# Attention, gated block and top-2 experts on one core: PV in threes, 400 slots per expert, and unequal early parts

## The chip, the cores and the metric

The kernel runs on one core of a Trainium2 chip. The metric is the device time of one execution in microseconds, as the median of several runs. Three executions of the kernel before took 881.61, 883.17 and 885.46 us.

## The reference, cut to what matters

Three blocks follow each other. Every matmul works on 32-bit values; weights and activations are split into a rounded high part and a low remainder, so that a product costs three matmuls (high x high, low x high or high x low, in the order the kernel chooses).

```python
# 1. attention, 2 x 8 heads, 768 positions, 64 wide; a score counts only within a hash bucket
scores = where(q_bucket == k_bucket, scale * q @ k.T, -1e9)
attn = exp(scores - max); attn /= sum(attn) + 1e-9
x = attn @ v                                   # 1536 tokens x 512
# 2. gated block, 512 -> 2048 -> 512
h = x @ w_in; x = (h * clip(h + 3, 0, 6) / 6) @ w_out
# 3. top-2 of 8 experts, 512 -> 1024 -> 512
noisy = x @ w_gate + log1p(exp(x @ w_noise)) * noise
for e in range(8):
    out[mask] += weight * (relu(x[mask] @ w1[e]) @ w2[e])   # mask: tokens with e in their top 2
```

`w_in` and `w_out` come as 64-bit floats.

## The kernel before, in words

TensorE (PE), VectorE (DVE), ScalarE (ACT) and GpSimd (POOL) carry out their instructions in the order of the program, which is written out by hand; SyncE (SP) issues most DMAs, also in that order, as soon as the buffer that a DMA writes is free. So the order of the Python loops is the order on each engine.

**Attention** (about 0 to 244 us). Two heads are worked on together, in 8 pairs p, each in two half-blocks of queries (`hb`), each with 6 key tiles of 128. The main loop (L609) runs over 96 steps g; 12 steps are a pair, 6 a half-block. Step g issues the scores of step g + 1 (`scores`, L470: for each of two heads two 384-wide matmuls into a tile "S", of which there are two, and an exponential on ACT into one of four tiles E), between them two or three `maxes` (L430: matmuls into one of two double tiles "mx", then a DVE reduce), and in every odd step the products with V of two key tiles (`av`, L482: 24 small matmuls each with half of the array's columns). After that come, in this order: the loads and splits of later pairs, the sum of V (`v_sum`, L324, at the ninth step of a pair: a POOL memset, then a DVE reduce), one step of the conversion, the weights of the next block, and what was deferred to this step (`at`, `run_deferred`): the stabiliser's transpose, eviction and DMA (`stab2`, L459, from the ACT queue, behind the third step of a half-block), the V-sum matmul (`v_sum2`), the uniform term (`uniform`, POOL), and the end of a half-block (`finish`).

**Conversion** (`conv`, L188). The 64-bit weights are turned into 32-bit ones in 32 pieces, 16 of them in attention: a load c_raw into a buffer of tag "wr", three steps later two ACT passes and a DVE pass, then DVE and POOL, DVE, and a store. Its buffers are those of the weights: "wr", "wh" and "wl", three each. `conv_step` (L670) moves every started piece by one stage and starts a new one where g % 6 == 3. The first three weight tiles are loaded in steps 84 to 86 (L676) and cast in 88 to 91.

**Gated block** (244 to 523 us). 48 units (3 chunks of 512 tokens x 16 slices of 128 hidden columns). A unit loads 512 KB of weights (`w_load`), casts them (`w_hi`, ACT) and takes the rest (`w_lo`, DVE), multiplies (`gemm1`, 12 matmuls; `gemm2`, 12 matmuls of 512 columns). Gates and top 2 are worked out per chunk (`routing`), and each token's row of 516 floats is scattered to a slot of its expert in DRAM (`xg`).

**Experts.** The slots of expert e are rows of `xg`, CAP of them. An expert has 8 units of 128 hidden columns with 512 KB of weights each. `PARTS` (L30) lists the work in order: expert, first slot, slots, row tiles, swapped or not. Experts 0 and 1 have an early part whose slots are filled by the first two chunks, so that it can run while the third chunk is routed (this stretch, 523 to 583 us, is called the passage); the rest of their slots comes last. A swapped part (`sw`) keeps weights stationary in the second layer too: 12 + 12 matmuls a unit as wide as the part has slots, into four banks (two tiles "S"), then four copies into `yt` and transposes back (`e_back`, four per row tile). A part that is not swapped has in the second layer, for each row tile, three matmuls of 512 columns a unit into half of one tile "S", and `e_out` scales the result and adds it to the output by a scattering DMA. In that form, the second row tile's matmuls of the last unit write the same tile that the first's `e_out` reads. `e_load`, `e_meta`, `e_trans` gather, read and transpose the slots of the next part in given units of the one before (`EL1`, L1074); expert 2's gather is issued by POOL, in column pieces, after the third chunk's scatter; later ones by SP at the first unit of the part before. If an expert got more than CAP rows, a block at the end (L1097) works off the rest.

Of the kernel before, what the change touches and what calls it, by code (L numbers as in the profile page):

```python
# [8 lines left out]
F32 = mybir.dt.float32  # L9
# [7 lines left out]

BIG = float(2 ** 33)
HALF = float(2 ** 32)
CAP = 416  # L20
EARLY = (224, 224)
ROW = 516
PF = (8, 2)
NU = 16
NS = 2
CL = 3
SL = CAP // 4
ROUTE = [(3, 0, 0), (1, 1, 0), (0, 1, 0), (5, 0, 0)]
NQ = len(EARLY)
PARTS = ([(e, 0, n, 2, False) for e, n in enumerate(EARLY)] + [(e, 0, CAP, 4, True) for e in range(NQ, 8)]  # L30
         + [(e, n, CAP - n, 2, False) for e, n in enumerate(EARLY)])
FSPLIT = 7
XA = 5
QJ = (1, 5)
# [10 lines left out]
def chain_kernel(ctx, tc, kq, vP, proj, wm, we, wgn, noise, out, dbg=None):  # L45
# [237 lines left out]
    with actx:  # L283
# [12 lines left out]
        def at(g, f, *a):  # L296
            defer.setdefault(g, []).append((f, a))
# [184 lines left out]
        def av(g):  # L482
            p, qh, kt = g // (2 * KT), g // KT % 2, g % KT
            t = T[p]
            if kt == 0:
                t["av"] = ps.tile([128, 512], F32, name="o", tag="o", bufs=1)
            for h in range(2):
                for i in range(KT // 2):
                    c = (h * (KT // 2) + i) * VW
                    for r in (0, 64):  # L490
                        nc.tensor.matmul(t["av"][r:r + 64, c:c + VW],  # L491
                                         E[g % NE][:, h, i * 128 + r:i * 128 + r + 64], t["V"][:, kt, h],
                                         start=kt == 0 and h == 0 and i == 0, stop=kt == KT - 1,
                                         tile_position=(0, r), skip_group_check=True)
            if kt == 0:
                at(g + 1, uniform, 2 * p + qh)
            elif kt == KT - 1:
                at(g + 1, finish(p, qh, t["av"]))

# [103 lines left out]
            elif i == 7:  # L603
                low_q(1)
        v_sum(0, False)
        at(0, v_sum2, 0)
        pend = []
        soon = []
        for g in range(G):  # L609
            p, j = divmod(g, 2 * KT)  # L610
            hb, st = divmod(g, KT)
            ahead = done[0] - ((hb + 2) * NI + 2 * st)
            todo = more(3 if ahead < 0 else 2, hb + 3)
            for hbd in pend:
                stab(hbd)
            pend2, pend = pend, []
            sc = scores(g + 1) if g + 1 < G else iter(())
            for k in range(2):
                next(sc, None)
                if todo:  # L620
                    m = todo.pop(0)
                    maxes(*m)
                    if m[1] == NI - 1:
                        pend.append(m[0])
                while soon:
                    f = soon.pop()
                    f[0](*f[1:])
            next(sc, None)
            if g in XG:
                x_split(0, [XG.index(g)])  # L630
            if g == G - 1:
                m1_first(0)
            if g % 2:
                av(g - 1)
                av(g)
            while todo:
                m = todo.pop(0)
                maxes(*m)
                if m[1] == NI - 1:
                    pend.append(m[0])  # L640
            for hbd in pend2:
                d = 2 if hbd > 2 else 0
                at(g + d, stab2, hbd)
            if p + 2 < NP:
                if j == 0:
                    load_cast(p + 2)
                elif j == 4:
                    bits_all(p + 2)
                    soon.append((bits_all2, p + 2))
                    at(g + 1, bits_all3, p + 2)  # L650
                    move_q(p + 2)
                elif j in (6, 7):
                    lows(p + 2, j - 6)
                elif j == 8:
                    move_mask_all(p + 2)
            if p + 1 < NP:
                if j == QJ[0]:
                    with tc.issue_after(T[0]["nrd"].ins):
                        move_qx(p + 1)
                elif j == QJ[1]:  # L660
                    move_k(p + 1)
            if p >= 1 and p + 1 < NP and j == 2:
                load_v(p + 1)
            if p + 1 < NP and j == 8:
                v_sum(p + 1)
                at(g + 3, v_sum2, p + 1)
            if p + 3 < NP and j == 6:
                load_raw(p + 3)
            if dbg is None or "x" not in dbg:
                conv_step(1 if g % 6 == 3 and cvn[0] < NU else 0, None, True)  # L670
            if g == 14:
                moe_consts()
            elif g == 16:
                moe_gate(f_p)
            if G - 12 <= g < G - 9:
                w_load(g - G + 12)  # L676
            elif g in WG:
                k = WG.index(g)
                (w_hi, w_lo)[k % 2](k // 2)
            run_deferred(g)  # L680
# [16 lines left out]
    def gemm2(y, k, gh, gl, m, first, last, ts=range(4)):  # L697
        wh, wl = W[k][1][:, 512:], W[k][2][:, 512:]
        for t in ts:
            o = y[t // 2][:m, t % 2, :]  # L700
            c = slice(t * m, (t + 1) * m)
            nc.tensor.matmul(o, gh[:, c], wh, start=first, stop=False)  # L702
            nc.tensor.matmul(o, gh[:, c], wl, start=False, stop=False)  # L703
            nc.tensor.matmul(o, gl[:, c], wh, start=False, stop=last)  # L704

    def m1_second(u):
        c, ft = plan[u]
        if ft in (0, FSPLIT):
            ys["y", c] = [ps.tile([128, 2, 512], F32, name="S", tag="S", bufs=2) for _ in range(2)]
        gh, gl = ys.pop(("g", u))  # L710
        y = ys["y", c]
        gemm2(y, u, gh, gl, 128, ft in (0, FSPLIT), ft in (FSPLIT - 1, 15))
        W.pop(u)
        if ft == FSPLIT - 1:
            if c < 2:
                ye = ys["ye", c] = x_rows(c)
            else:
                ye = ys["ye", c] = m_p.tile([128, 4, ROW], F32, name="ye", bufs=1)
            nc.scalar.copy(ye[:, 0:2, 0:512], y[0])
            nc.scalar.copy(ye[:, 2:4, 0:512], y[1])  # L720
        elif ft == 15:
            for i in range(2):
                yd = ys["ye", c][:, 2 * i:2 * i + 2, 0:512]
                nc.vector.tensor_tensor(yd, y[i], yd, op=ALU.add)
# [209 lines left out]
    def m2_second(v):  # L934
        q, ft = divmod(v, 8)
        e, s0, n, nt, sw = PARTS[q]
        if ft == 0:
            ex["y", q] = [ps.tile([128, 2, 512], F32, name="S", tag="S", bufs=2) for _ in range(2 if sw else 1)]
        hh, hl = ex.pop(("h", v))
        y = ex["y", q]  # L940
        if not sw:
# [3 lines left out]
            for t in range(nt):  # L945
                gemm2(y, NMU + v, hh, hl, n // nt, ft == 0, ft == 7, (t,))
                if ft == 7:
                    e_out(q, t, y[0][:, t, :])
        else:
            wh, wl = W[NMU + v][1:]  # L950
            for d in range(4):
# [235 lines left out]
```

## Time and profile before

| | us |
|---|---|
| median of three runs | 883.17 |
| profiled execution, its own time | 878.66 |
| its span | 876.8 |
| TensorE busy | 829.8 (95%) |
| weight loads into TensorE | 717.1 (82%) |
| VectorE busy | 524.4 (60%) |
| ScalarE busy | 422.2 (48%) |
| GpSimd busy | 214.5 (24%) |

The profile tells of one execution. TensorE's matmuls are pipelined: the time of one in a row is longer than the step from one start to the next, so the price of a matmul is read from two starts. In a timeline a row gives start, duration, engine, line, operation, out<-in, shape and count; brackets give the idle time before it and what ended it. Several matmuls of one kind in a row are merged into one row.

### The profile page before, as it was taken

The page shows a single profiled execution, that of the slowest core. Times are in us where ns is not written, and L with a number is a line of the kernel's source. Part 1 is how long each engine was busy: PE and PEld are TensorE (multiplying, and loading weights), DVE is VectorE, ACT ScalarE, POOL GpSimd, SP SyncE. Part 2 cuts the span into 40 slices and gives each one's busy share as a digit, 9 for nine tenths or more (in the row PEclk, how much of TensorE's full clock was granted, in tenths as well). Part 3 has the DMA queues.
Part 4 walks back from the last instruction along what each step waited for, and adds up shares of the span by engine and source line. Part 5 has one row for each costly group of instructions (what it writes and reads, how often), then busy time and mean ns, then how long its engine had stood idle before and what let it go on. Part 6 is the DMA issues. An engine that isn't in the chain of part 4 may idle for free.

```text
span 876.8 us, 15979 instructions
## 1 busy us (share of the span) xinstructions
PE 829.8 (95%) x6313; PEld 717.1 (82%) x6313; DVE 524.4 (60%) x865; ACT 422.2 (48%) x714; POOL 214.5 (24%) x244
## 2 busy tenths in 40 slices
PE   7899999999799999999999999989999999999993
PEld 3677788788678888888878787879999999999982
DVE  7678777777356776645556557555445444544651
ACT  5455455456446666644444444443444444343551
POOL 6345444343211311100040124410112020211211
PEclk9999999999899999999999999999999999999997
DMA  8667668661345799862252265973565555645661
GB/s 259 174 187 211 185 161 235 170 177 56 117 156 188 221 319 317 302 229 97 73 184 90 92 207 164 293 203 124 152 169 134 162 131 164 136 147 145 174 196 22
DMA packets 52348, 151.75 MB, mean 173 GB/s; under 512 B 8741, under 2 KB 9661, under 8 KB 52265
## 3 DMA queue, kind: packets, MB, share of 16 engines
q1 hardware_dynamic: 44393, 131.02, 48.3%
q0 software_dynamic: 7648, 19.53, 10.2%
q8 instruction: 51, 0.84, 0.4%
q14 instruction: 32, 0.26, 0.1%
q10 hardware_dynamic: 224, 0.10, 0.0%
HBM read 105.89 MB, written 32.41 MB: 158 GB/s over the span
## 4 chain that ended last, share of the span: by engine, by line
PE 79%; DVE 8%; DMA 3%; issue 3%; ACT 3%; POOL 2%; POOLq 0%; ACTq 0%; SPq 0%; DVEq 0%
PE mx L260 28%; PE o L491 7%; PE S L702 5%; PE S L704 5%; PE S L703 5%; PE S L954 4%; PE S L955 4%; PE S L956 4%; PE S L477 4%; PE mx L440 3%; PE S L478 3%; DVE mc L444 2%; DVE wl L238 1%; DVE vr L329 1%; ACT wh L232 1%
## 5 line engine op out<-in xcount | busy, mean ns | idle before, releaser
L238 DVE TENSOR_TENSOR wl<-wr,wh 128x1024 fp32r<-128x1024 f32 (+1 forms) x128 | 155.6, 1216 | 126.6 <-ACT wh L232 124.9
L232 ACT CAST wh<-wr 128x1024 fp32r<-128x1024 f32 x128 | 134.3, 1049 | 123.8 <-PE S L956 75.6
L479 ACT ACTIVATE E<-S 128x384 f32<-128x384 f32 x192 | 90.3, 491 | 82.5 <-PE S L478 76.7
L444 DVE TENSOR_REDUCE mc<-mx 128x1 f32<-128x768 f32 x96 | 90.3, 953 | 32.8 <-PE mx L440 32.8
L982 POOL DMA_INDIRECT out_dram<-ot,ti x28 | 44.1, 1575 | 234.9 <-ACT ot L981 186.1
L276 DVE SCALAR_TENSOR_TENSOR g<-t,mx 128x512 f32<-128x512 f32 x47 | 32.4, 689 | 94.6 <-ACT t L275 94.6
L702 PE MATMUL S<-wh,gh 128*128 128x512 f32 (+1 forms) x208 | 82.1, 395 | 1.1 <-ACT xh L919 1.1
L491 PEld LDWEIGHTS o<-V,E 128*64 128x64 f32 x2304 | 72.7, 140 | 12.3 <-issue 9.6
L477 PE MATMUL S<-QX,KS 128*128 128x384 f32 x192 | 75.7, 394 | 6.2 <-ACT E L479 6.0
L704 PE MATMUL S<-wh,gl 128*128 128x512 f32 (+1 forms) x208 | 81.1, 390 | 0.0
L703 PE MATMUL S<-wl,gh 128*128 128x512 f32 (+1 forms) x208 | 81.0, 389 | 0.0
L491 PE MATMUL o<-V,E 128*64 128x66 f32 x2304 | 79.4, 226 | 0.0
L440 PE MATMUL mx<-B,A 128*128 128x384 f32 x192 | 64.6, 349 | 11.8 <-DVE mc L444 9.3
L954 PE MATMUL S<-hh,wh 128*128 128x416 f32 x192 | 70.7, 368 | 0.0
L955 PE MATMUL S<-hh,wl 128*128 128x416 f32 x192 | 67.5, 352 | 0.0
L956 PE MATMUL S<-hl,wh 128*128 128x416 f32 x192 | 67.4, 351 | 0.0
L478 PE MATMUL S<-A,B 128*128 128x384 f32 x192 | 65.6, 342 | 1.4 <-DMA A<-mr 1.4
L929 ACT ACTIVATE hh<-mx 128x416 fp32r<-128x416 f32 (+2 forms) x72 | 33.0, 459 | 66.1 <-PE mx L260 65.7
L260 PE MATMUL mx<-xh,wh 128*128 128x512 f32 (+1 forms) x252 | 61.8, 367 | 2.8 <-ACT wh L232 2.8
L260 PE MATMUL mx<-xh,wl 128*128 128x512 f32 (+1 forms) x252 | 60.8, 363 | 1.8 <-DVE wl L238 1.6
L275 ACT ACTIVATE t<-mx,half 128x512 f32<-128x512 f32 x47 | 32.3, 688 | 59.2 <-PE mx L260 59.2
L260 PE MATMUL mx<-xl,wh 128*128 128x512 f32 (+1 forms) x252 | 60.2, 360 | 0.0
(247 smaller groups left out, 1588.9 us busy)
## 6 DMA issues: line engine op xcount, KB each, us to landing
wr<-in_we_dram SPq DMA_DIRECT2D x80, 512.0 KB
wr<-w SPq DMA_DIRECT2D x48, 512.0 KB
c_raw<-in_wm_dram SPq DMA_DIRECT2D x32, 512.0 KB
xg<-pt SPq DMA_DIRECT2D x8, 838.5 KB
raw<-in_kq_dram SPq DMA_DIRECT2D x8, 768.0 KB
B<-in_kq_dram POOLq DMA_DIRECT2D x7, 768.0 KB, 9.7
xr<-xg SPq DMA_DIRECT2D x5, 838.5 KB
w<-c_ta SPq DMA_DIRECT2D x16, 256.0 KB
```

The lines of the kernel that those rows point to most:

```text
L232: nc.scalar.copy(hi, W[k][0])
L238: nc.vector.tensor_tensor(lo[:, :n], W[k][0][:, :n], W[k][1][:, :n].bitcast(F32), op=ALU.subtract)
L260: nc.tensor.matmul(h, a[:, d * 128:(d + 1) * 128], b[:, d], start=i == 0 and d == 0, stop=i == 2 and d == 3)
L444: nc.vector.tensor_reduce(t["mc"][:, c:c + 1], pm[:, :, :QW], axis=AX.XY, op=ALU.max)
L477: nc.tensor.matmul(s[:, :QW], t["KS"][:, h, ks], t["QX"][:, qh, qs], start=True, stop=False)
L491: nc.tensor.matmul(t["av"][r:r + 64, c:c + VW], E[g % NE][:, h, i * 128 + r:i * 128 + r + 64], t["V"][:, kt, h], start=kt == 0 and h == 0 ...
L702: nc.tensor.matmul(o, gh[:, c], wh, start=first, stop=False)
L703: nc.tensor.matmul(o, gh[:, c], wl, start=False, stop=False)
L704: nc.tensor.matmul(o, gl[:, c], wh, start=False, stop=last)
L954: nc.tensor.matmul(o, wh[:, ds], hh, start=ft == 0, stop=False)
L955: nc.tensor.matmul(o, wl[:, ds], hh, start=False, stop=False)
L956: nc.tensor.matmul(o, wh[:, ds], hl, start=False, stop=ft == 7)
```

## The change

PV is done for three key tiles in a row, in the third and sixth step of a half-block (`AV`); `uniform` moves with it, from the second to the third step. The first `v_sum2` moves from step 0 to step 1. A conversion starts every five steps instead of six, still 16 in attention. CAP falls from 416 to 400 (and the 104 partitions of whole-expert tiles to 100). Expert 0's early part keeps 224 slots; expert 1's has 128 in one row tile. At the end comes expert 1 with 272 slots, swapped, in four row tiles of 68, and after it expert 0 with 176 slots in two. In parts that are not swapped the first row tile accumulates in a tile "S", a second one in a bank of tag "mx", of which there are four.

```diff
-CAP = 416
-EARLY = (224, 224)
+CAP = 400
+EARLY = (224, 128)
...
+AV = 3
 SL = CAP // 4
...
-PARTS = ([(e, 0, n, 2, False) for e, n in enumerate(EARLY)] + [(e, 0, CAP, 4, True) for e in range(NQ, 8)]
-         + [(e, n, CAP - n, 2, False) for e, n in enumerate(EARLY)])
+PARTS = ([(0, 0, EARLY[0], 2, False), (1, 0, EARLY[1], 1, False)] + [(e, 0, CAP, 4, True) for e in range(NQ, 8)]
+         + [(1, EARLY[1], CAP - EARLY[1], 4, True), (0, EARLY[0], CAP - EARLY[0], 2, False)])
...
             if kt == 0:
-                at(g + 1, uniform, 2 * p + qh)
+                at(g + AV - 1, uniform, 2 * p + qh)
...
-        at(0, v_sum2, 0)
+        at(1, v_sum2, 0)
...
-            if g % 2:
-                av(g - 1)
-                av(g)
+            if g % AV == AV - 1:
+                for i in range(g - AV + 1, g + 1):
+                    av(i)
...
-                conv_step(1 if g % 6 == 3 and cvn[0] < NU else 0, None, True)
+                conv_step(1 if g % 5 == 3 and cvn[0] < NU else 0, None, True)
...
         for t in ts:
-            o = y[t // 2][:m, t % 2, :]
+            o = y[t][:m]
...
-        gemm2(y, u, gh, gl, 128, ft in (0, FSPLIT), ft in (FSPLIT - 1, 15))
+        gemm2([i[:, j] for i in y for j in range(2)], u, gh, gl, 128, ft in (0, FSPLIT), ft in (FSPLIT - 1, 15))
...
         if ft == 0:
-            ex["y", q] = [ps.tile([128, 2, 512], F32, name="S", tag="S", bufs=2) for _ in range(2 if sw else 1)]
+            y = [ps.tile([128, 2, 512], F32, name="S", tag="S", bufs=2) for _ in range(2 if sw else 1)]
+            if not sw:
+                y = [y[0][:, 0]] + [ps.tile([128, 512], F32, name="mx", tag="mx", bufs=MX) for _ in range(nt - 1)]
+            ex["y", q] = y
...
-                    e_out(q, t, y[0][:, t, :])
+                    e_out(q, t, y[t])
```

## Rows read from the trace of the kernel before

**Rows 1.** The page: TensorE's granted clock in 40 slices, tenths of full speed.

```profile
PEclk9999999999899999999999999999999999999997
```

**Rows 2.** Busy us by stage: length, PE, PEld, DVE, ACT, POOL; clock, DMA share, GB/s.

```profile
108.50:135.10 26.60, 25.45 (x383) 21.14 (x382) 20.49 (x28) 14.42 (x32) 11.95 (x19) 1.00 0.70 194
...
235.00:236.00 1.00, 1.00 (x4) 0.68 (x4) 0.72 (x1) 0.62 (x2) 0.18 (x1) 0.50 0.47 123
...
552.90:583.10 30.20, 27.01 (x173) 22.73 (x172) 15.93 (x26) 13.56 (x22) 6.51 (x7) 1.00 0.90 243
583.10:813.00 229.90, 229.90 (x1297) 225.95 (x1296) 112.89 (x168) 93.23 (x138) 35.60 (x23) 1.00 0.57 149
```

**Rows 3.** Timeline of TensorE in the expert stage.

```profile
803.59 0.91 PE L260 MATMUL mx<-xth,wh 128*128 128x416 f32 x4
...
805.85 0.33 PE L918 MATMUL mx<-ident,xr 96*128 96x96 f32 x2
...
840.91 0.47 PE L702 MATMUL S<-wh,hh 128*96 128x512 f32 x1 [0.77 <-ACT ot L981]
...
841.68 0.58 PE L260 MATMUL mx<-xth,wh 128*128 128x192 f32 x4
...
843.00 0.39 PE L702 MATMUL S<-wh,hh 128*96 128x512 f32 x1
...
844.38 0.58 PE L260 MATMUL mx<-xth,wh 128*128 128x192 f32 x4
```

**Rows 4.** Timeline of TensorE in attention and just after it.

```profile
109.92 0.33 PE L478 MATMUL S<-A,B 128*128 128x384 f32 x1
...
110.62 0.34 PE L440 MATMUL mx<-B,A 128*128 128x384 f32 x1
110.89 1.62 PE L491 MATMUL o<-V,E 128*64 128x66 f32 x48
112.44 0.44 PE L477 MATMUL S<-QX,KS 128*128 128x384 f32 x1
...
113.70 0.44 PE L477 MATMUL S<-QX,KS 128*128 128x384 f32 x1
...
233.53 0.69 PE L477 MATMUL S<-QX,KS 128*128 128x384 f32 x1 [4.85 <-ACT E L479]
...
236.75 2.38 PE L491 MATMUL o<-V,E 128*64 128x66 f32 x48
...
251.47 1.21 PE L260 MATMUL mx<-xh,wh 128*128 128x512 f32 x4 [1.44 <-ACT wh L232]
```

**Rows 5.** Timeline of ScalarE in the passage.

```profile
572.07 1.04 ACT L232 CAST wh<-wr 128x1024 fp32r<-128x1024 f32 x1 [4.56 <-DMA wr<-in_we_dram]
```

**Rows 6.** Timeline of SyncE at the end of attention.

```profile
227.29 5.23 SPq L191 DMA_DIRECT2D c_raw<-in_wm_dram  x2
```

**Rows 7.** Timeline of ScalarE in attention.

```profile
110.00 0.65 ACT L202 ACTIVATE c_lu<-c_raw 128x512 int32<-128x512 uint32 x1
...
111.12 0.86 ACT L479 ACTIVATE E<-S 128x384 f32<-128x384 f32 x2
113.16 1.03 ACT L479 ACTIVATE E<-S 128x384 f32<-128x384 f32 x2 [1.18 <-PE S L478]
...
114.36 0.62 ACTq L468 DMA_DIRECT2D A<-mr  x1
...
230.91 0.69 ACT L202 ACTIVATE c_lu<-c_raw 128x512 int32<-128x512 uint32 x1 [4.45 <-DMA c_raw<-in_wm_dram]
```

**Rows 8.** TensorE's waits, 28 to 214 us: total, times, longest.

```profile
PE mx L440 <- DVE mc L444: 7.2, 6, 1.7
```

**Rows 9.** Timeline of VectorE in attention: the sum of V.

```profile
129.88 1.60 DVE L329 TENSOR_REDUCE vr<-V 128x132 f32<-128x792 f32 x1 [1.44 <-POOL V L327]
```

**Rows 10.** Busy time by stretches of 1 us: gathers of 104 and of 96 partitions.

```profile
732.00:733.00 1.00, 1.00 (x9) 0.94 (x8) 0.50 (x2) 0.61 (x2) 0.00 (x0) 1.00 0.84 173
...
769.50:770.50 1.00, 1.00 (x7) 0.99 (x6) 0.00 (x0) 0.90 (x1) 0.00 (x0) 1.00 1.01 367
```

## The prediction

> **What bounds the kernel now.** I read the clock line of the page first, then the busy time by stage, then the order of TensorE's instructions inside each stage the change touches. The clock stands at full speed but for one slice [rows 1]. In the six whole experts (583 to 813 us) TensorE is busy all the time, so there a shorter matmul is a shorter kernel [rows 2]. In a middle attention period of twelve steps it is busy 25.5 of 26.6 us and VectorE 20.5 [rows 2]. In the passage (expert 1's early part, 552.9 to 583.1) it is busy 27.0 of 30.2 us while the DMA engines stand at 0.90: there TensorE waits for weights [rows 2]. The end of attention has a hole of its own.
>
> **Six experts, 416 to 400 slots.** Twelve 416-wide matmuls run from 803.59 to 805.85, 188 ns each; four 384-wide steps run from 109.92 to 110.62, 175 ns each [rows 3, 4]. So 16 columns are worth 6.7 ns. Each expert has 8 units of 24 such matmuls: 1152 x 6.7 ns = **-7.7 us**, all on the path. Weight casts and hidden-layer evictions run beside it. With the reference's inputs the experts get 364 to 396 rows, so 400 slots hold them and no overflow block runs.
>
> **The end, experts 1 and 0.** Before, two parts of 192 slots: 12 narrow matmuls take 841.68 to 843.00 (110 ns each), six 512-wide ones 843.00 to 844.38 (230 ns), so 2.70 us a unit, 43.2 for 16 [rows 3]. 192 columns do not go below 110 ns although the slope above would give 95: a floor. After, 176 slots lie on the same floor: 8 x 2.70 = 21.6. Expert 1's late part becomes 24 matmuls of 272 columns a unit. From the 175 ns at 384 the slope gives 128 ns, the floor 110; the line is nearer, since 128 is above the floor, so 8 x 24 x 128 ns = 24.6 (bound 21.1). Being swapped it is also transposed back: 16 transposes, about 0.11 us each, 1.7, and its gather needs 8 more small transposes, 0.4. On the other side, a second row tile now has a PSUM tile of its own: before, it waited for the first one's eviction (0.77 us idle and the 0.39 of a matmul where a step is 0.23: 0.93 lost), four times in the kernel, twice here [rows 3]: -1.9. Sum: 46.2 - 43.2 + 1.7 + 0.4 - 1.9 = **+3.2 us**. The gathers of the two last parts change places on SyncE, each still issued one part ahead.
> The Trainium skill ("TensorE: Matmul & The Clock Gate", Back-to-back issue gap) gives N/2.4 + 2.5 ns per warm matmul, 116 ns at 272 columns; the sum would be 2.3 us lower by it. The trace disagrees: 188 ns at 416 and 175 at 384, where the formula has 176 and 163, so I keep the line.
>
> **The passage.** Expert 1's early part drops from two row tiles to one: 24 wide matmuls fewer, 24 x 0.23 = 5.5 us if TensorE set the pace. It doesn't: ScalarE waits 4.56 us for the weights of the last unit and starts the cast at 572.07 [rows 5]. As many weights must come, and the loads of expert 2 wait for the last scatter as before, so I take this arrival as fixed. What is left is what comes after it: the second layers of the last two units (2 x 0.69) and an eviction wait like the one above (0.93) [rows 3]: **-2.3 us**; bounds 0 and -5.5. The eviction wait at the end of expert 0's early part vanishes too, but only to wait longer for weights: 0. Holding one of the four "mx" banks for that part leaves three; a unit uses two in 2.7 us and each is read within about 1 us, so 0.
>
> **The end of attention.** The last two conversions start at steps 87 and 93, while the first three weight tiles want the same three buffers. SyncE can issue the load c_raw only at 227.29; ScalarE waits 4.45 us for it at 230.91 with the exponentials queued behind; TensorE then idles 4.85 us, comes back at a granted clock of 0.50, the 1.2 GHz level (48 PV matmuls take 2.38 us against 1.62), and later waits 1.44 us for the third weight tile [rows 2, 4, 6, 7]. With a start every 5 steps the 16th conversion starts at step 78 and is stored at 87, ahead of the casts at 88; SyncE gets the same loads and stores, closer together. Removed: 4.85 + 1.44 + about 1.9 for two steps at half clock (estimate from that block and scores half as fast) = **-8.2 us**. What is late next: the second weight cast of 1.05 us comes at a step without PV followed by another, +0.8.
>
> **The middle of attention** (steps 2 to 83). Five things.
> (a) Entering PV costs 0.27 us (110.62 to 110.89) instead of 0.175 [rows 4]. Leaving it isn't shown apart; between nothing and the same again, I take the same. 16 blocks fewer of 48, some 14 of them here: -2.7.
> (b) Two score tiles rotate. In a step without PV the exponentials begin 0.72 us after the step's first matmul (112.44, 113.16), and the next step's first score waits for the first of them: a step takes 1.26 us where six matmuls and the slower first one need 1.15 [rows 4, 7]. There are 64 such steps instead of 48: +1.
> (c) The stabiliser's eviction and its DMA issue (0.62 us) sit on ScalarE behind step 2 of a half-block [rows 7]. Before, a PV step followed and hid it. Now two steps without PV follow: the issue ends 1.28 us (114.98) after the step's first score (113.70) [rows 4, 7], some 0.1 earlier where ScalarE is idle before it, and an exponential would start after 0.72: it starts 0.46 to 0.49 late and the next step waits. 12 half-blocks: +5.9; zero if ScalarE caught up.
> (d) A conversion's two ScalarE passes (110.00 to 111.12) always fell behind an even step, ahead of a PV step [rows 7]. With a period of 5 against 6 they visit all positions; in two of six (6 conversions) two steps without PV follow: the passes end some 2.9 us into the first (exponentials done at 1.7, then the passes), where the next exponentials are due at 1.26 + 0.72, so TensorE waits about 0.95: +5.7; zero to 10.
> (e) Once in 12 steps VectorE's sum of V waits 1.44 us for a POOL memset behind POOL's share of the conversion, and maxes then wait for reduces: 7.2 us in six waits [rows 8, 9]. Now the sum falls behind a PV step of some 3.5 us, the uniform term comes after the memset, and the conversion isn't locked to it: -6.9; bounds 0 and -7.2.
> Sum -2.7 + 1 + 5.9 + 5.7 - 6.9 = **+3.0 us**, bounds -9 and +10. The V-sum matmul moved out of step 0 frees TensorE while VectorE stays late: -1 (0 to -2).
>
> **Sum**: -7.7 + 3.2 - 2.3 - 8.2 + 0.8 + 3.0 - 1.0 = -12.2 us. The profiled execution took 878.66 us (span 876.8), so 866.5; the median of the runs, 883.17, lies 4.5 us above it, and I carry the difference: **871.0 us**.
>
> **Rivals.**
> 1. The new ScalarE delays don't show: c and d at zero, the middle at -8.6, total -24: 859. For: ScalarE is busy only 14.4 of 26.6 us [rows 2]. Against: its queue is in order and the two score tiles leave no slack [rows 7]. Chance 0.13.
> 2. The weights of the passage come earlier because TensorE releases buffers sooner: -5.5 there, 868. For: a load starts when a split ends. Against: the DMA engines are full [rows 2]. It shares the forecast's outcome; 0.12.
> 3. Slower: VectorE becomes the bound of attention. It has 20.5 us of work in 26.6 [rows 2], and 1.1 more by the denser conversions. If it could not use the four long PV stretches of a period, 2 us each, a period would take 21.6 + 8 = 29.6, 3.0 more; seven periods +21, in place of the middle's +3.0, so 889. It decides where reduces can't run two tiles behind the maxes. Against: each reduce takes 0.96 of a 1.26 us step. Chance 0.05.
> 4. The hole at the end of attention stays, because another load holds the weight buffers: +7.4, 878. Chance 0.1.
> 5. Expert 1's late gather has 68 partitions. During a 104-partition gather the DMA engines are 0.84 busy at 173 GB/s, during a 96-partition one 1.01 at 367 [rows 10]: a gather doesn't use them all. Were it on a quarter of them, at 140 KB an engine instead of 65 KB in about 6 us, it would take 13 us and hold up the weights queued behind it, of which three units are in flight: some 3 us late, 874. Chance 0.08. The Trainium skill ("DMA: Bandwidth & Descriptors", How many engines (k)) says that the partition count must divide by the number of engines used: 13 for 104, 10 for 100, 4 for 68; the share of 0.84 agrees with 13 of 16.
>
> **How the numbers follow.** The forecast itself has 0.52, around 866 to 876. With rivals 2, 4, 5 and part of 1, 860 to 878 holds about 8 in 10; outside lie the better half of rival 1 and rival 3. A change under 0.5% (4.4 us) is about what a measurement of this kernel can't tell from none. Faster by more: rivals 1, 2, 5, half of 4 and the forecast but for 0.03, 0.87. Within it: that 0.03 and the other half of 4, 0.08. Slower: rival 3, 0.05.
>
> **What would show it.** Right: no idle above 2 us between steps 84 and 95 and a full clock there; a unit of experts 2 to 7 0.16 us shorter (24 x 6.7 ns); expert 1's early part some 2.3 us shorter with ScalarE still waiting for weights; 272-wide matmuls near 128 ns; PV blocks of 72; after steps 3 of half-blocks a wait of about 0.5 us on the exponentials; maxes hardly waiting for reduces. Wrong: VectorE busy over 85% in the middle periods, an expert period unchanged, or weights waited for beside the 68-partition gather.

## The result, and the profile after

The changed kernel took 872.87 us (median of 8 runs, 869.03 to 880.01), the kernel before 883.4 (8 runs, 880.2 to 886.49): a ratio of 0.9884, interval 0.9856 to 0.9913, 10.5 us less. The forecast was 871.0. The profiled executions differ by less: 878.66 before, 872.92 after. The one of before lay 4.7 us under its median, the one of after lies on its own.

First the page of the changed kernel: the busy times and the clock line that answers to [rows 1].

```profile
PE 825.2 (95%) x6357; PEld 719.0 (83%) x6357; DVE 516.8 (59%) x867; ACT 424.3 (49%) x717; POOL 217.0 (25%) x245
...
PEclk8899999999999999999999999989999999999998
```

The dip at the end of attention (slice 10, counted from 0) is gone. New ones stand in the first two slices and in the passage (slice 26). Lines of the code have moved by 1, and by 4 from the experts' second layer on: L441 is the maxes' matmul, L478 and L479 the score matmuls, L480 the exponential.

Then the time by stretch, in both traces and in a second profile of the kernel before (an experiment below). A step begins with its first score matmul; in the experts a stretch begins where ScalarE starts on a unit's hidden layer:

| us | before | before, again | after | forecast of the change |
|---|---|---|---|---|
| to step 6 | 40.6 | 38.9 | 41.5 | -1.0 (start) |
| steps 6 to 83 | 173.2 | 174.3 | 179.3 | +3.0 (middle) |
| steps 84 to 93 | 25.2 | 24.6 | 19.2 | -8.2 + 0.8, with the next line's 1.44 |
| on to expert 0's first eviction | 285.1 | 287.7 | 286.5 | |
| expert 0's early part | 24.5 | 24.5 | 24.3 | 0 |
| passage, to expert 2's second unit | 37.0 | 37.0 | 34.9 | -2.3 |
| six experts, 46 of their 48 units | 225.2 | 225.2 | 218.1 | -7.4 (46/48 of -7.7) |
| on to the last matmul | 52.4 | 52.4 | 54.6 | +3.2 |
| after it | 13.6 | 13.6 | 12.7 | |

Busy time in four of these stretches of the changed kernel: an attention period of twelve steps, steps 84 to 93, the passage, the six experts (length, PE, PEld, DVE, ACT, POOL; clock, DMA share, GB/s).

```profile
111.69:139.95 28.26, 25.95 (x382) 20.97 (x382) 19.91 (x30) 15.80 (x34) 10.97 (x14) 1.00 0.72 203
220.76:239.94 19.18, 16.66 (x263) 13.19 (x262) 5.84 (x10) 11.00 (x25) 5.18 (x4) 1.00 0.20 71
550.67:585.58 34.91, 30.04 (x176) 25.93 (x175) 18.38 (x32) 15.94 (x28) 10.71 (x11) 0.90 0.94 269
585.58:803.67 218.09, 218.09 (x1280) 216.19 (x1279) 109.37 (x165) 90.70 (x135) 31.98 (x22) 1.00 0.57 151
```

Against [rows 2]: the period is 1.66 us longer at only 0.5 us more of TensorE, so TensorE waits there now, while VectorE is no busier. The end of attention runs at full clock. In the passage the clock is 0.90 and the DMA engines are as full as before.

**What TensorE waits for in attention.** TensorE, then ScalarE, where two steps without PV follow the stabiliser (steps 14 to 16).

```profile
59.13 2.33 PE L492 MATMUL o<-V,E 128*64 128x66 f32 x72
61.39 0.28 PE L466 MATMUL z<-ident,nr 128*12 128x128 f32 x1
61.42 0.42 PE L478 MATMUL S<-QX,KS 128*128 128x384 f32 x1
...
63.22 0.45 PE L478 MATMUL S<-QX,KS 128*128 128x384 f32 x1 [0.51 <-ACT E L480]
```

```profile
61.70 0.26 ACT L468 CAST mr<-z 12x128 fp32r<-12x128 f32 x1 [2.08 <-PE z L466]
61.98 0.64 ACTq L469 DMA_DIRECT2D A<-mr  x1
62.67 0.87 ACT L480 ACTIVATE E<-S 128x384 f32<-128x384 f32 x2 [0.72 <-PE S L479]
```

The score is ready at about 62.0, the exponential starts at 62.67, and the next step's score waits for it: 1.80 us from 61.42 to 63.22 where such a step takes 1.20. All twelve half-blocks of steps 12 to 83 show it. A conversion two steps ahead of PV does the same (step 37): ScalarE's two passes stand between two pairs of exponentials.

```profile
113.23 0.66 ACT L203 ACTIVATE c_lu<-c_raw 128x512 int32<-128x512 uint32 x1
113.78 0.66 ACT L204 ACTIVATE c_lu<-c_raw 128x512 f32<-128x512 f32 x1
114.35 0.85 ACT L480 ACTIVATE E<-S 128x384 f32<-128x384 f32 x2
```

The sum of V still waits for its memset, at its worst in step 20. First VectorE, then GpSimd, then TensorE three steps later.

```profile
77.38 1.60 DVE L330 TENSOR_REDUCE vr<-V 128x132 f32<-128x792 f32 x1 [3.82 <-POOL V L328]
```

```profile
72.89 1.82 POOL L362 TENSOR_TENSOR KS<-raw,B 128x768 fp32r<-128x768 f32 x1
74.67 0.83 POOL L512 TENSOR_TENSOR x_all<-ov,r 128x384 f32<-128x384 f32 x1
75.45 1.83 POOL L362 TENSOR_TENSOR KS<-raw,B 128x768 fp32r<-128x768 f32 x1
77.22 0.13 POOL L328 MEMSET V<- 128x24 f32 x1
```

```profile
80.51 0.61 PE L441 MATMUL mx<-B,A 128*128 128x384 f32 x1 [1.39 <-DVE mc L445]
...
82.01 3.25 PE L492 MATMUL o<-V,E 128*64 128x66 f32 x72
```

A 0.13 us memset stands behind two subtractions of 1.8 us, VectorE stands still behind it with the reduces queued, and TensorE, after its wait, does 72 PV matmuls in 3.25 us instead of 2.33: at the lower clock.

TensorE's waits, 28 to 214 us, first before, then after, to be read with [rows 8] (total, times, longest):

```profile
PE S L477 <- ACT E L479: 0.6, 2, 0.3
```

```profile
PE S L478 <- ACT E L480: 8.4, 14, 1.7
PE mx L441 <- DVE mc L445: 2.4, 4, 1.4
```

The waits for reduces fell from 7.2 us to 2.4; those for exponentials rose from 0.6 to 8.4.

**The experts.** Steps of TensorE at 400, 272 and 176 columns.

```profile
799.66 0.34 PE L958 MATMUL S<-hh,wh 128*128 128x400 f32 x1
799.83 0.34 PE L959 MATMUL S<-hh,wl 128*128 128x400 f32 x1
800.02 0.34 PE L960 MATMUL S<-hl,wh 128*128 128x400 f32 x1
800.20 0.34 PE L958 MATMUL S<-hh,wh 128*128 128x400 f32 x1
...
805.97 0.66 PE L261 MATMUL mx<-xth,wh 128*128 128x272 f32 x4
806.47 0.67 PE L261 MATMUL mx<-xth,wl 128*128 128x272 f32 x4
...
836.50 0.61 PE L261 MATMUL mx<-xth,wl 128*128 128x176 f32 x4
836.95 0.61 PE L261 MATMUL mx<-xtl,wh 128*128 128x176 f32 x4
```

Three matmuls from 799.66 to 800.20 give 180 ns (182 in the median of all 400-wide steps); four in 0.50 us give 125 ns at 272 columns; four in 0.45 give 112 at 176, the floor.

**The passage**, ScalarE and TensorE, with the wait that answers to [rows 5].

```profile
571.56 1.05 ACT L233 CAST wh<-wr 128x1024 fp32r<-128x1024 f32 x1 [3.75 <-DMA wr<-in_we_dram]
```

```profile
575.67 1.53 PE L919 MATMUL mx<-ident,xr 100*128 100x100 f32 x8
578.41 1.70 PE L261 MATMUL mx<-xth,wh 128*128 128x400 f32 x4 [1.20 <-DVE xtl L921]
579.91 1.53 PE L261 MATMUL mx<-xth,wl 128*128 128x400 f32 x4
```

The weights are still waited for, and later TensorE takes 0.33 us for a 400-wide matmul (1.33 us for four, 579.91 to 581.24): the lower clock. Two waits of before do not come back, those of a second row tile for the eviction of the first. TensorE before:

```profile
552.09 0.48 PE L702 MATMUL S<-wh,gh 128*112 128x512 f32 x1 [1.08 <-ACT xh L919]
...
582.34 0.48 PE L702 MATMUL S<-wh,hh 128*112 128x512 f32 x1 [0.78 <-ACT x_all L981]
```

The view puts the first down to a cast of ScalarE; the eviction behind that cast (L981) ran from 551.35 to 552.04.

### The profile page after: what moved, and what is told of

The parts are those of the page before. It is cut to its first block, busy times and chain, and to the rows that moved or that the text cites. A ratio compares the mean times of both kernels' runs of the same rounds, so it can differ in the third digit from the quotient of the medians.

```text
span 871.0 us, 16078 instructions
## 1 busy us (share of the span) xinstructions
PE 825.2 (95%) x6357; PEld 719.0 (83%) x6357; DVE 516.8 (59%) x867; ACT 424.3 (49%) x717; POOL 217.0 (25%) x245
## 5 line engine op out<-in xcount | busy, mean ns | idle before, releaser
L480 ACT ACTIVATE E<-S 128x384 f32<-128x384 f32 x192 | 90.8, 492 | 61.9 <-PE S L479 58.6
L986 POOL DMA_INDIRECT out_dram<-ot,ti x30 | 47.9, 1597 | 228.1 <-ACT ot L985 177.2
L478 PE MATMUL S<-QX,KS 128*128 128x384 f32 x192 | 75.6, 394 | 12.1 <-ACT E L480 12.0
L958 PE MATMUL S<-hh,wh 128*128 128x400 f32 (+1 forms) x224 | 79.4, 354 | 0.0
L704 PE MATMUL S<-wl,gh 128*128 128x512 f32 (+1 forms) x200 | 78.4, 392 | 0.0
L492 PE MATMUL o<-V,E 128*64 128x66 f32 x2304 | 75.7, 225 | 0.0
L959 PE MATMUL S<-hh,wl 128*128 128x400 f32 (+1 forms) x224 | 75.3, 336 | 0.0
L960 PE MATMUL S<-hl,wh 128*128 128x400 f32 (+1 forms) x224 | 74.8, 334 | 0.0
L441 PE MATMUL mx<-B,A 128*128 128x384 f32 x192 | 66.4, 360 | 8.2 <-DVE mc L445 4.3
L479 PE MATMUL S<-A,B 128*128 128x384 f32 x192 | 66.1, 344 | 1.6 <-DMA A<-mr 1.6
L261 PE MATMUL mx<-xh,wl 128*128 128x512 f32 (+2 forms) x252 | 60.8, 363 | 2.9 <-DVE wl L239 2.8
L478 PEld LDWEIGHTS S<-QX,KS 128*128 128x128 f32 x192 | 36.7, 191 | 32.3 <-ACT E L480 29.7
L930 ACT ACTIVATE hh<-mx 128x400 fp32r<-128x400 f32 (+3 forms) x72 | 32.2, 447 | 63.9 <-PE mx L261 63.7
L261 PE MATMUL mx<-xh,wh 128*128 128x512 f32 (+2 forms) x252 | 61.6, 366 | 0.8 <-ACT wh L233 0.8
```

The source lines that it names most:

```text
L261: nc.tensor.matmul(h, a[:, d * 128:(d + 1) * 128], b[:, d], start=i == 0 and d == 0, stop=i == 2 and d == 3)
L478: nc.tensor.matmul(s[:, :QW], t["KS"][:, h, ks], t["QX"][:, qh, qs], start=True, stop=False)
L480: nc.scalar.activation(E[g % NE][:, h], s[:, :QW], ACTF.Exp, scale=0.125)
L492: nc.tensor.matmul(t["av"][r:r + 64, c:c + VW], E[g % NE][:, h, i * 128 + r:i * 128 + r + 64], t["V"][:, kt, h], start=kt == 0 and h == 0 ...
L958: nc.tensor.matmul(o, wh[:, ds], hh, start=ft == 0, stop=False)
L959: nc.tensor.matmul(o, wl[:, ds], hh, start=False, stop=False)
```

## The experiments

**The kernel before, again.** No edit.

> The kernel before once more, nothing changed, for a second look at where its executions differ. Its profiled execution took 878.66 us and the median of its runs is 883.4; that of the changed kernel lies on its median (872.9). Theory 1: the profile shown of before was a good execution; a second one is 3 to 6 us longer (882 to 885), and the time lies where TensorE waits for a DMA and then runs at the lower clock: the start (20 to 32 us) and the gather of expert 0's slots at 518 us (0.96 us of waiting before, 2.13 and ten matmuls at 0.43 us each in the changed kernel: 2.75 us). The gather stretch then gives some 2.75 more. Theory 2: the 2.75 us there belong to the change (its gathers or loads collide): the second profile of before again has under 1.2 us of waiting and full clock at the gather, and is within 1.5 us of 878.7.

Measured: 882.94 us against 884.57, ratio 0.9991 (0.9963 to 1.0018). Its profiled execution took 879.81 us, only 1.2 more than the first, so a second one is not 3 to 6 us longer. But at the gather of expert 0's slots it does what the changed kernel does. TensorE there:

```profile
518.65 0.99 PE L918 MATMUL mx<-ident,x_all 112*128 112x112 f32 x8 [2.01 <-DMA x_all<-xg]
...
520.18 0.63 PE L704 MATMUL S<-wh,gl 128*128 128x512 f32 x1
520.61 0.63 PE L702 MATMUL S<-wh,gh 128*128 128x512 f32 x1
```

After 2.01 us of waiting a 512-wide matmul takes 0.43 us instead of 0.23 until 522.7; the changed kernel waits 2.13 and does the same. Ten other profiles wait 0.96 to 1.7 us there, and the matmuls behind take 0.23 (the two kernels with the edit to this gather, below, do not wait). So the 2.75 us lost there belong to the execution, not to the change.

**Conversions every five steps, alone** (in the kernel before).

```diff
-                conv_step(1 if g % 6 == 3 and cvn[0] < NU else 0, None, True)
+                conv_step(1 if g % 5 == 3 and cvn[0] < NU else 0, None, True)
```

> The kernel before with a conversion started every five steps instead of six, nothing else. Theory 1 (the prediction): this alone takes the hole at the end of attention away: no idle over 2 us between steps 84 and 95, no clock of 0.50 there, -7.4 us from step 84 to the second gated unit, and with PV in pairs ScalarE's passes stay covered (each step without PV is followed by one with it), so the whole is 6 to 9 us faster (ratio about 0.991). Rival: the buffers are only taken by another load (the loads of the weights move with the conversions); the hole stays, within 2 us of before.

Measured: 874.18 us, ratio 0.9881 (0.9845 to 0.9918): this one line gives what the whole change gives. Steps 84 to 93 of it, busy time and clock:

```profile
215.68:234.19 18.51, 17.60 (x287) 14.17 (x287) 5.92 (x10) 11.19 (x25) 6.32 (x9) 1.00 0.29 100
```

18.5 us instead of 25.2, at full clock, with no wait over 0.3 us; with the 1.44 us wait after it gone too, -8.1. Theory 1 holds for the end of attention. What it did not say: steps 6 to 83 take 177.0 us instead of 173.2, since the denser conversions still leave the sum of V behind its memset (step 23: 6.0 us, step 47: 6.3).

**PV for two key tiles, the rest as changed.**

```diff
-AV = 3
+AV = 2
```

> The changed kernel with PV for two key tiles again (AV = 2), everything else as changed. Theory 1: PV in threes is a loss, since two steps without PV follow each other: the stabiliser's eviction and DMA issue delay the exponentials by 0.58 us in each of 12 half-blocks (7.0), and five conversions by 0.7 to 1.85 (5.5); against 2 us of fewer changes of form. With pairs, attention (to step 94) is 8 to 11 us shorter and the kernel 862 to 865 us (ratio to the kernel before about 0.977). Theory 2 (what the change seems made for): grouping pays by the fewer changes of form, and the delays would come in pairs as well: the kernel becomes 2 to 4 us slower, 875 to 877.

Measured: 873.21 us, ratio 0.9864 (0.9832 to 0.9896): as the changed kernel, where theory 1 had 862 to 865 and theory 2 875 to 877. The waits that theory 1 names are gone in its profile (the steps behind the stabiliser take 1.20 to 1.26 us, conversions delay nothing). But the start took 45.7 us, and the sum of V cost more: steps 23 and 47 took 7.4 and 7.0 us, with a wait of 2.6 and 2.1 for a reduce and the PV behind it at the lower clock. Steps 6 to 83: 178.1 against 179.3.

**The old parts at 400 slots.**

```diff
-EARLY = (224, 128)
+EARLY = (224, 224)
...
-         + [(1, EARLY[1], CAP - EARLY[1], 4, True), (0, EARLY[0], CAP - EARLY[0], 2, False)])
+         + [(e, n, CAP - n, 2, False) for e, n in enumerate(EARLY)])
```

> The changed kernel with the early parts of 224 slots each and the late parts of 176 slots each, not swapped, expert 0 first, as before; CAP stays 400, PV in threes, conversions every five steps, the second row tile in its own bank. It undoes the unequal parts alone. Theory 1 (the prediction, by its terms): the end becomes shorter, since two parts of 176 lie on the floor of 110 ns (2 x 21.6 us) instead of 272 columns at 125 ns plus transposes: about -5 (24.0 - 21.6 + 1.7 + 0.4); the passage gets back its 24 wide matmuls but is held by the weights: +1.4 to +5.5. Together 0 +- 4 us: 869 to 876. Rival: the passage is bound by TensorE once the weights come earlier (they came 2.8 us earlier relative to the last scatters in the changed kernel), so the full +5.5 and the lower clock stays as it is: 873 to 876 with the passage over 36 us. Third: fewer gathered rows (96 x 2 KB less) are what brings the weights earlier; then the last cast of the passage starts some 1 us later again.

Measured: 870.13 us, ratio 0.9812 (0.9768 to 0.9857). From expert 7's last eviction to the last matmul 50.2 us instead of 54.6; the passage 35.2 instead of 34.9. Over all profiles the passage takes 34.9 to 37.5 us with one row tile of expert 1 (six) and 35.0 to 35.8 with two (five). So the smaller early part buys nothing in the passage, and the late part of 272 slots costs 4.5 us: theory 1's direction, with the lower bound of the passage. What one row tile spares TensorE may be lost again at the clock: granted in the passage were 0.73 to 0.91 in the six profiles with one tile, 0.95 to 1.00 in the five with two. Whether it would be shorter at full clock no run shows.

**The stabiliser ahead of PV** (in the changed kernel).

```diff
+            if g in mid:
+                stab2(mid.pop(g))
             if g % AV == AV - 1:
...
-                at(g + d, stab2, hbd)
+                    mid[g + 2] = hbd
```

> The changed kernel with the stabiliser's transpose, eviction and DMA issue put ahead of the PV of the third step of a half-block instead of behind it (from the second pair's half-blocks on). Theory 1: behind PV they fall into two steps without PV, and the exponentials come 0.58 us late (step 15, 21, 27 and so on take 1.78 instead of 1.20); ahead of PV, 2.3 us of matmuls cover them. 12 half-blocks: 7 us, so 864 to 868, and those steps at 1.20. Rival: the transposes then wait for GpSimd's four small instructions, the wait stands ahead of PV instead, and the time stays within 2 us of the changed kernel.

Measured: 875.83 us, ratio 0.9875 (0.9833 to 0.9916): nothing gained. The steps named do take 1.20 us instead of 1.78, for 0.1 us more in each PV step, as theory 1 has it. Steps 6 to 83 still take 177.8 us (179.3 before this edit): the last steps of pairs of heads lose up to 1.7 us to reduces, and steps 29, 41 and 53 now take 0.4 to 0.7 us more than such a step without waits, with waits for the row that the stabiliser writes. The rival's cause, a wait for GpSimd ahead of PV, comes once (0.22 us). The start took 45.2.

**Conversions placed ahead of PV.**

```diff
-                conv_step(1 if g % 5 == 3 and cvn[0] < NU else 0, None, True)
+                conv_step(1 if g % 15 in (4, 10, 13) and cvn[0] < NU else 0, None, True)
```

> The changed kernel with the 16 conversions started at steps 4, 10 and 13 of every 15 instead of 3, 8 and 13: as many, but the two ScalarE passes of each (three steps after its start) now always stand in the step ahead of one with PV. Theory 1: the waits of 0.7 to 1.85 us on the exponentials in steps 7, 22, 37, 67 and 82 are gone (5.5 us); GpSimd's share never stands right ahead of the sum of V, so its waits get shorter too: 5 to 8 us less, 865 to 868. Rival: what is late in those steps is the sum of the exponentials and the stabiliser, and the passes only move: under 2 us of change.

Measured: 885.65 us, ratio 0.9996 (0.9967 to 1.0024): 13 us lost, and both theories are wrong. The waits of steps 22, 37, 67 and 82 are gone and step 7's is halved, so the cause was named rightly. But steps 6 to 83 take 191.6 us. TensorE's and VectorE's waits, 28 to 214 us:

```profile
DVE vr L330 <- POOL V L328: 11.8, 3, 4.1
...
PE mx L441 <- DVE mc L445: 7.8, 5, 3.0
PE S L479 <- DMA A<-mr: 6.6, 4, 2.9
```

The likely cause was not tried apart: conversions three steps apart put their shares of GpSimd and VectorE, and their 512 KB loads, beside the sum of V and the stabiliser's row.

**The memset of V earlier.**

```diff
+            if p + 1 < NP and j == 5:
+                nc.gpsimd.memset(T[p + 1]["V"][:, :, :, 64:], 1.0)
...
-                v_sum(p + 1)
+                v_sum(p + 1, False)
```

> The changed kernel with GpSimd's memset of the ones in V issued at the sixth step of a pair instead of the ninth, ahead of its two subtractions of 1.83 us (KS), not behind. Theory 1: VectorE's sum of V waited 3.8, 2.4 and less for that memset in steps 20 to 23, 44 to 47 and 68 to 71, and the reduces behind it held TensorE (3.4, 0.9 and 1.0 us over a plain last step of a pair, the first with the clock at 0.50): 4 to 6 us less, 867 to 869, no wait of VectorE on GpSimd over 0.5 us. This is the term of the prediction that failed (-6.9 for the sum of V). Rival: the memset waits for the load of V, holds GpSimd, and the subtractions are late instead: no gain.

Measured: 875.9 us, ratio 0.9869 (0.9821 to 0.9917). The last steps of all pairs of heads take 3.74 to 3.96 us (6.94, 4.38 and 4.48 in steps 23, 47 and 71 of the changed kernel), and VectorE waits for GpSimd no more. Yet steps 6 to 83 take 181.4: another wait has moved in. ScalarE, then TensorE at step 29:

```profile
89.58 0.62 ACTq L469 DMA_DIRECT2D A<-mr  x1
```

```profile
92.85 0.44 PE L478 MATMUL S<-QX,KS 128*128 128x384 f32 x1
94.81 0.44 PE L479 MATMUL S<-A,B 128*128 128x384 f32 x1 [1.52 <-DMA A<-mr]
95.09 0.44 PE L441 MATMUL mx<-B,A 128*128 128x384 f32 x1
95.33 0.52 PE L478 MATMUL S<-QX,KS 128*128 128x384 f32 x1
```

The row of 6 KB that the stabiliser writes, issued at 89.58, is needed at 93.1; its last packet ends at 93.8, and the matmul starts at 94.81. There are three such waits, 3.8 us in all, two with the lower clock behind them. So theory 1 is right on the cause and wrong on the gain.

**The first V-sum matmul in step 0.**

```diff
-        at(1, v_sum2, 0)
+        at(0, v_sum2, 0)
```

> The changed kernel with the first V-sum matmul in step 0 again. So far step 6 began at 40.6, 38.9 and 38.7 us in three profiles with it in step 0 (all PV in pairs) and at 41.5, 45.7 and 44.9 in three with it in step 1. Theory 1 (the prediction): moving it frees TensorE for a microsecond; undoing it costs 0 to 1 us, and the spread is that of DMAs landing: step 6 anywhere between 39 and 46. Theory 2: the move is what costs: the waits for VectorE's sum and for the masks' DMA then stand in one piece in step 1 (2.9 to 7.3 us) instead of two, TensorE drops to the lower clock for the scores and the PV behind; with it in step 0 again step 6 begins before 41, and the kernel is 2 to 4 us faster (869 to 871).

Measured: 875.38 us, ratio 0.9896 (0.9832 to 0.996); step 6 begins at 39.6 us. That looked like theory 2, but over all 14 profiles step 6 begins at 38.7 to 46.1 us with the matmul in step 0 (eight) and at 41.5 to 45.7 with it in step 1 (six). The medians, 40.1 and 44.3 us, lean to theory 2, but two of the eight begin at 45.2 and 46.1. What the move is worth stays open.

**What these point to.** The old parts, PV for two key tiles ("pairs"), the memset earlier and the matmul in step 0, as edited above, in one kernel.

> What the runs so far point to, in one kernel: 400 slots, early parts of 224 as before, conversions every five steps, PV for two key tiles, the memset of V ahead of GpSimd's subtractions, the first V-sum matmul in step 0. Worked out from the profiles by stretch: to step 6 39.5 us (as in four profiles with the matmul in step 0), steps 6 to 23 38 (41.9 less the waits for the sum of V), 24 to 83 127 to 131 (135.2 less 8.3 of such waits and of clock behind them, plus up to 4 if the stabiliser's DMA is late, as it was when the memset was moved), 84 to the end of PV 23.6, then as in the kernel with the old parts: 848 to 853 span, 850 to 856 us, ratio about 0.963. Rival (PV in threes is worth its price): with pairs the waits move to the stabiliser's DMA (step 29, 41, 53 over 1 us each), and the kernel comes out at 862 to 866, no better than the next one.

Measured: 867.4 us (857.8 to 870.96), ratio 0.9794 (0.9743 to 0.9845). The profiled execution took 859.37: steps 6 to 83 174.4 us, with the stabiliser's row as the last large wait. TensorE's waits, 28 to 214 us, then one of them:

```profile
PE S L479 <- DMA A<-mr: 6.1, 6, 2.2
```

```profile
147.30 0.44 PE L479 MATMUL S<-A,B 128*128 128x384 f32 x1 [2.19 <-DMA A<-mr]
```

Two of six runs lie 2 to 3 us above the 850 to 856 expected, four 9 to 15; where these lose it no profile shows. The rival's waits came, over 1 us each at steps 29 and 53, though not at 41.

**The same with PV for three key tiles** ("threes"), and the stabiliser ahead of PV.

> The same with PV for three key tiles and the stabiliser ahead of PV in the third step. Theory 1: two steps without PV in a row leave five conversions uncovered (1.0 us each) and the stabiliser's 6 KB row less time to land (4.2 us from issue to use where pairs give 4.9, and up to 4.9 us of it were needed): 856 to 861, 4 to 8 us behind pairs. Theory 2: with the stabiliser covered, threes save 0.15 us a half-block and are as fast: within 2 us of pairs.

Measured: 869.3 us (863.81 to 872.95), ratio 0.9839 (0.9801 to 0.9876). In the profiles steps 6 to 83 take 177.8 us against 174.4, with 0.8 us lost in each of steps 22, 37 and 67 to conversions and 9.6 us in step 53, where the row came 3.3 us late. The medians leave it open; the profiles speak for pairs.

**Half a unit ahead of the gather's transposes** (in the kernel with pairs; `m1_second` takes the row tiles to do).

```diff
+            m1_second(u, range(2))
             for d in range(4):
                 e_trans(0, d)
-            m1_second(u)
+            m1_second(u, range(2, 4))
```

> The kernel with pairs, and in the last unit of the gated block half of the second layer's matmuls (six of 227 ns, 1.36 us) ahead of the transposes of expert 0's gathered slots, half behind. Theory 1: TensorE waited 0.96 to 2.1 us for that gather in six profiles, and where it waited 2.0 or more ten matmuls ran at the lower clock behind it (2.75 us in all): the wait shrinks by 1.36 us and the clock stays up: 1 to 3 us faster than pairs. Rival: the evictions of the transposes, covered by 2.7 us of matmuls so far, are covered by 1.36 only, and the first layer of expert 0 waits for them instead: no gain, or 1 us lost.

Measured: 860.76 us (855.39 to 862.13), ratio 0.9724 (0.9691 to 0.9758), the best kernel of the study. TensorE no longer waits for the gather:

```profile
515.59 0.39 PE L707 MATMUL S<-wh,gl 128*128 128x512 f32 x1
515.83 0.93 PE L924 MATMUL mx<-ident,x_all 112*128 112x112 f32 x8
```

In the profiles it is worth 1.4 us, of which expert 0 gives 0.7 back; that no run here takes the 865 to 871 us of four runs of the kernel with pairs is more than this explains.

**The row earlier still** (in the last kernel).

```diff
-                at(g + d, stab2, hbd)
+                    mid[g + 1] = hbd
```

> The last kernel (pairs, half of a unit ahead of the gather's transposes) with the stabiliser's transpose, eviction and 6 KB DMA in the second step of a half-block, ahead of its PV, instead of behind the third step: issued about 3 us earlier, and covered by PV on ScalarE. Theory 1: since the sum of V no longer holds anybody, it is this row, 3.6 to 6.4 us from issue to landing where a pair's operands (768 KB of B, V, KS) are loaded at the same time and 1.45 elsewhere, that holds the second score matmul of steps 17, 29, 53 and 77 (0.82, 1.97, 2.09 and 1.59 us, 6.5 in all): all four waits go, steps 24 to 83 take 128 to 130 us instead of 134, and the kernel comes out at 853 to 857 (ratio about 0.967). Rival: the row lands when the big loads have passed, whenever it is issued: it is issued among the same loads, the waits shrink by less than half, 859 to 861. Second rival: TensorE now waits for GpSimd's four small instructions ahead of PV (over 0.5 us in each half-block), and nothing is gained.

Measured: 871.01 us, ratio 0.987 (0.9833 to 0.9906): 10 us worse than without it. The waits of steps 29, 53 and 77 are gone, that of step 17 is not. ScalarE and TensorE in step 32:

```profile
101.52 0.24 ACT L468 CAST mr<-z 12x128 fp32r<-12x128 f32 x1
105.28 0.62 ACTq L469 DMA_DIRECT2D A<-mr  x1
```

```profile
107.60 0.69 PE L478 MATMUL S<-QX,KS 128*128 128x384 f32 x1 [3.46 <-ACT E L480]
```

The issue itself now stands 3.5 us in ScalarE's queue with the exponentials behind it (four DMAs into the same tile A, issued from 100.19 on, are the likely cause; not tried apart), and where GpSimd's four instructions are late TensorE waits ahead of PV (three times, 3.9 us). Neither the first theory nor the rival holds; the second rival does in part.

## Why the prediction was right, and where it was not

The forecast of the change was -12.2 us; the medians give -10.5, the two profiles -5.8. The 4.5 us between the profile of before and its median were carried over whole, while the profile of after lies on its median. Two large terms, the six experts and the end of attention, were right. The other errors of the pair of profiles are +3.1 us in the middle, +2.8 at the gather of expert 0's slots, +1.8 at the start and -1.9 at the end. The gather and the start vary as much between executions; without those two the pair gives -10.4, with the middle and the end partly cancelling. So the mechanism was right in its large terms, and that the sum came within 2 us of the medians is in part luck.

- **Six experts, -7.7:** measured -7.1 over 46 units, 0.154 us a unit where 0.16 were forecast. A 400-wide step is 182 ns, 6 under 416.
- **End of attention, -8.2 + 0.8:** measured -6.0 in steps 84 to 93 and -1.44 behind them, so -7.4 as forecast; the one-line experiment gives -8.1. What the changed kernel loses beside it is 0.5 us at the second cast (step 91, forecast 0.8) and one more wait behind the stabiliser (step 87, 0.58), less what threes save.
- **The end, +3.2:** +2.2 to the last matmul, less 0.9 behind it. 272 columns took 125 ns (forecast 128). The formula of the Trainium skill ("TensorE: Matmul & The Clock Gate", Back-to-back issue gap) has 116, and the trace does not agree with it. Against the old parts at 400 slots the unequal ones cost 4.5 us here.
- **The passage, -2.3:** the size was right (-2.1), the reason failed. "The second layers of the last two units" brought nothing: the old early parts run as short a passage. Weights still end the waits, and TensorE, idle more, fell to the lower clock. What both forms share, beside 400 slots, is the second row tile's own bank: TensorE's two waits for an eviction (1.08 and 0.78 us, 1.9 in all) are gone in every profile with it. The prediction counted one of them at 0.93 and put the other at nothing. Over all profiles the passage takes 37.0 to 38.2 us with 416 slots and 34.9 to 37.5 with 400, so the 2.1 of the one pair has a spread of its own size.
- **The middle, +3.0:** measured +6.1. (c) 12 waits of 0.58 instead of 0.46 to 0.49: +7.0 for +5.9. (d) five conversions, 5.2 us for 5.7. (a) and (b): a half-block without waits went from 12.1 to 11.9 us, -2.7 over 13, for -1.7. The term that failed is (e), "the uniform term comes after the memset, and the conversion isn't locked to it: -6.9". Over a last step of a pair of heads without waits (3.05 us before, 3.75 after), the seven of steps 11 to 83 lost 8.7 us before and 4.5 after: -4.2. TensorE's waits for reduces say much the same, 7.2 us before and 2.4 after. What stood ahead of the memset was not the conversion alone but the two subtractions of 1.8 us, which the list of (e) left out. Steps 29, 41, 44 and 56 take some 1.5 us more than their like, partly in waits for the stabiliser's row. These terms come to 6.8; the difference to 6.1 was not followed.
- **The start, -1:** +0.8 in this profile, inside a spread of 7.4 us over 14 profiles; such a term can't be read from one pair.
- **Rivals.** Of 1 nothing showed: ScalarE's delays are all there. Of 2 the profile has a part: the last cast began 0.5 us earlier (571.56, [rows 5]), though the last unit of expert 0 was 2.1 later; the lower clock gave it back. 4 and 5 did not come: the hole closed, and TensorE waits for no weights beside the 68-partition gather. 3 did not decide here (VectorE 19.9 of 28.3 us). With conversions three steps apart TensorE waited 7.8 us for reduces, but behind a VectorE that itself waited 11.8 us for GpSimd.

## What to carry to other kernels

A wait that goes uncovers the one behind it: in this attention loop the memset, the stabiliser's row and the exponentials stand one behind the other, and the edits that took one away showed another. Take a change of several parts apart before believing its sum: one line gave all of this one's gain, one part cost 4.5 us, and a version without that part, with pairs and with the two covered waits, is 2.8% faster than the kernel before where the change is 1.2%. Whether grouping pays depends on what stands uncovered between the groups: here a half-block without waits was 0.2 us shorter with threes, and each wait behind the stabiliser took 0.58. Between the kernels called pairs and threes the medians leave it open.

## What was not expected of the hardware

- **A small DMA among large ones.** The 6 KB row lands 1.4 to 1.7 us after its issue when little else moves. Where the next pair's operands are loaded, its first packet starts up to 6.0 us after the issue, and it is complete after up to 8.2.
- **A short wait costs twice.** At the gather a wait of 2.0 or 2.1 us was followed by some ten 512-wide matmuls at 0.43 us instead of 0.23, with a granted clock of 0.50, the 1.2 GHz level; in ten other profiles, with waits of 0.96 to 1.7 us there, the clock stayed at 1.00. In attention, 72 PV matmuls behind a wait of 1.39 us took 3.25 us instead of 2.33.
- **The start varies from execution to execution.** Two kernels with the same code up to step 6 began it at 41.4 and 46.1 us (pairs, and pairs with the gather's transposes moved), and all 14 profiles lie between 38.7 and 46.1. Most of it is step 1, which took 2.8 to 11.6 us; where it was long, TensorE waited up to 7.0 us for what the view puts down to the masks' DMA. A pair of profiles can't tell terms of that size there.
